# The layout of a transposed K tile: where the stride goes, into the copy or into the weight load

## The chip, the core and the metric

The kernel runs on one core of a Trainium2 chip. The metric is the device time of one execution in microseconds (us), the median of several runs. The profile of one execution stands beside it.

## The reference, cut to what matters

Two blocks, one behind the other. The first is a gated linear attention with complex gates, over 4 batches, 8 heads, 768 positions and 48 channels a head:

```python
scale = np.minimum(mag, 0.999) / (mag + 1e-06)      # mag = |a_re + i a_im|
for t in range(S):
    S_re, S_im = ar*S_re - ai*S_im + kv, ar*S_im + ai*S_re   # kv = k_t (outer) v_t
    y[:, :, t] = q_t @ S_re
```

The second is a multiplicative feed-forward block on the 3072 rows of 384 values that this gives: `h = ((x @ w1) * (x @ w2)) @ w3`, and `h @ w_out`. All is fp32.

## The kernel before, in words

**Units.** The 768 positions of a batch are cut in two halves of 384 (TT), so there are 8 units (NU). A unit has three chunks (UC) of 128 positions (C).

**Gates.** `gates(u)` computes the running products of the gates' magnitudes and the running sums of their angles by scans, and multiplies q and k with them. It leaves two tensors of rotated k: R holds the real part and K2 the imaginary part. In both, a partition is a pair (d, head), with 16 values of d and 8 heads side by side, and a column block f (three of them, KD) tells which third of a head's 48 channels is meant. From the same data, DMAs build QL and KL, which have the 96 values (d, real or imaginary, f) of one head down the partitions.

**States.** For a chunk's contribution to the state, the positions must lie down the partitions. `turn(u, c, x)` transposes the three blocks of R (x = 0) or K2 (x = 1) for chunk c on TensorE into one PSUM tile `tp` of 128 positions by (f, d, head), and ScalarE copies this into the SBUF tile KT (L654). Then `state(u, c)` multiplies, for each head, the 96 columns of KT that belong to it (the weights, 128 positions by 96) with 64 columns of V (the moving operand), into the PSUM tile `kv` (L702), and adds the state before to it (L707 or L709). The profile shows two instructions of a kind for each fp32 matmul or weight load of this product: a group of 8 heads is 16 loads and 16 matmuls. Where the state is needed further, `turn` and `state` are called for all three chunks of an even unit and for two of an odd one: 5 chunks for each batch, 20 in all, and 40 copies, one for each chunk and x.

**Outputs and feed-forward.** `scores` (L664) and `outputs` (L691) give the chunk's part of y, which is copied to `xT` (L693). `ffn_ab` multiplies xT with w1 and w2 (L722), and `ffn_out` (L738) multiplies their product with the fused matrix w3 w_out, which L852 makes at the start.

**Order.** TensorE's order is written by hand: `unit` and `pieces` deal the attention pieces of unit u out among the feed-forward matmuls of unit u - 1. The other engines' order comes from a scheduler; the copies of L654, L693, L727 have high priority in it. The unit's transposes come first, and a chunk's `state` comes one piece behind the second of its transposes.

**The layout that matters here.** KT is laid out before as (head, d, x, f). A head's 96 columns lie together, so the weight load of L702 reads 96 elements in a row. The copy of L654 goes through `tp` in its own order (f, d, head), the head innermost. In KT a step of one head is 96 elements, so every element of the write lies 384 bytes from the one before it.

Of the kernel before, what the change touches and what calls it, by code (L numbers as in the profile page):

```python
# [10 lines left out]
FP = mybir.dt.float32  # L11
# [363 lines left out]
def kernel(  # L375
# [36 lines left out]
    nc = tc.nc  # L412
    B, H, D, S = qt.shape
    P = 128
# [4 lines left out]
    KD = DM // P  # L419
    DG = P // H  # L420
# [25 lines left out]
    two = fast.enter_context(tc.tile_pool(name="two", bufs=2))  # L446
# [33 lines left out]
    g_t, L_t, xT_t, ab_t, T_t, KT_t = {}, {}, {}, {}, {}, {}  # L480
# [164 lines left out]
    def turn(u, c, x):  # L645

        src = L_t[u][2 + x]
        if x == 0:
            KT_t[u, c] = two.tile([P, H, DG, 2, KD], FP, tag="KT", name="KT")
        tp = ps_v.tile([P, KD, C], FP, tag="v", name="tp")  # L650
        for f in range(KD):
            nc.tensor.transpose(out=tp[:, f], in_=src[:, f, c * C:(c + 1) * C], identity=ident)  # L652
        with tc.high_priority():
            nc.scalar.copy(out=KT_t[u, c][:, :, :, x].rearrange("p h d f -> p f d h"),  # L654
                           in_=tp.rearrange("p f (d h) -> p f d h", h=H))

    def scores(u, c, x):
# [37 lines left out]
    def state(u, c):  # L695

        KT, V = KT_t.pop((u, c)), Vb[u % 2][:, c]
        n = u % 2 * UC + c
        T = T_t.get((u // 2, n))
        kv = ps_v.tile([2 * D, H, 64], FP, tag="v", name="kv")  # L700
        for hd in range(H):
            nc.tensor.matmul(out=kv[:, hd], lhsT=KT[:, hd].rearrange("p d x f -> p (d x f)"), rhs=V[:, hd],  # L702
                             start=True, stop=True)
        Tn = three.tile([2 * D, H, 64], FP, tag="T", name="T")
        with tc.high_priority():
            if T is None:
                nc.scalar.copy(out=Tn, in_=kv)  # L707
            else:
                nc.vector.tensor_tensor(out=Tn, in0=kv, in1=T, op=OP.add)  # L709
        if c == UC - 1:  # L710
            rho = L_t[u][1][:, :, TT:TT + 1].to_broadcast([2 * D, H, 64])
            nc.vector.tensor_tensor(out=Tn, in0=Tn, in1=rho, op=OP.mult)
        T_t[u // 2, n + 1] = Tn
# [170 lines left out]
    def pieces(u):  # L884

        sc = [[lambda c=c, x=x: scores(u, c, x) for x in range(2)] for c in range(UC)]
        tr = [[lambda c=c, x=x: turn(u, c, x) for x in range(2)] for c in range(UC)]
        kv = [lambda c=c: state(u, c) for c in range(UC)]
        y = [lambda c=c: outputs(u, c) for c in range(UC)]

        if u % 2:
            return [[tr[0][0]], [tr[0][1]], [tr[1][0], kv[0]], [tr[1][1]], [kv[1]], sc[0], sc[1] + [y[0]], sc[2] + [y[1]],
                    [y[2]]]
        return [[tr[0][0]], [tr[0][1]], [tr[1][0], kv[0]], [tr[1][1]], [tr[2][0], kv[1]], [tr[2][1]], [kv[2]] + sc[0],
                sc[1] + [y[0]], sc[2] + [y[1]], [y[2]]]
# [131 lines left out]
```

## Time and profile before

| what | value |
|---|---|
| time, median of 3 runs | 591.22 us (587.91 to 591.81) |
| span of the profiled execution | 591.2 us |
| TensorE busy | 556.7 us |
| ScalarE busy | 350.2 us |
| VectorE busy | 304.7 us |
| clock granted to TensorE, mean | 0.98 |

The profile's names: PE is TensorE, PEld its weight loads, which run beside the matmuls, ACT is ScalarE, DVE is VectorE, SPq the queue that issues the DMAs. L654 is line 654 of the kernel. A group row gives the line, the engine, the operation, the tiles (out<-in) and their shapes, the count, then the busy time in us, the mean of one in ns, and the engine's idle time just before with what ended it. The mean of one instruction on TensorE includes latency that the next one overlaps, so the pace of a row of matmuls is read from the chain of waits, in which each piece starts where the one that released it ends.

### The profile page before, as it was taken

The numbers are of one execution on the slowest core, as the hardware profiler recorded it, in microseconds if no ns is written. First come the engines' busy times: TensorE is split into PE (matmuls) and PEld (weight loads), VectorE is DVE, ScalarE is ACT, GpSimd is POOL, SyncE is SP. The second block draws the span as 40 slices with busy tenths as digits, with TensorE's granted clock in tenths as the row PEclk, the third lists the DMA queues.
The fourth block names the chain that finished last, engine by engine and source line by source line (L and its number), as shares of the span: only waits on it lengthen the run. The fifth ranks groups of instructions, "written<-read, shape, count | busy, mean of one in ns | idle before, by whom it ended". The sixth has DMA issues, their size and how long they took to land.

```text
span 591.2 us, 8844 instructions
## 1 busy us (share of the span) xinstructions
PE 556.7 (94%) x3514; PEld 367.3 (62%) x3514; DVE 304.7 (52%) x420; ACT 350.2 (59%) x572; POOL 5.3 (1%) x11
## 2 busy tenths in 40 slices
PE   4779989979899999999999999999999999999996
PEld 2335775558456765677567765776567756766553
DVE  6998488845761576158512674257415682300110
ACT  6897648566983698379835698498635742111100
POOL 3000000000000000000000000000000000000000
PEclk9779999989899999999999999999999999999999
DMA  8777999377385648652754347825920026000001
GB/s 294 271 280 221 250 287 287 108 183 213 121 234 117 185 137 240 130 173 85 194 120 105 124 141 177 247 73 157 206 76 1 14 67 121 1 15 29 0 1 44
DMA packets 46050, 84.71 MB, mean 143 GB/s; under 512 B 4656, under 2 KB 36144, under 8 KB 45104
## 3 DMA queue, kind: packets, MB, share of 16 engines
q1 hardware_dynamic: 46000, 84.06, 50.2%
q8 instruction: 29, 0.48, 0.3%
q14 instruction: 21, 0.17, 0.1%
HBM read 60.42 MB, written 4.72 MB: 110 GB/s over the span
## 4 chain that ended last, share of the span: by engine, by line
PE 66%; DMA 10%; ACT 9%; DVE 8%; SPq 4%; issue 2%; DVEq 0%; ACTq 0%
PE m L722 38%; PE o L738 13%; PE y L691 4%; PE sc L664 3%; PE f L852 3%; SPq L485 3%; PE kv L702 3%; DMA im<-in_a_im_dram 2%; ACT gZ L544 2%; DMA look<-in_w_dram 2%; PE tp L652 2%; DMA look<-in_a_re_dram 2%; DMA raw<-in_w_dram 1%; DMA vr<-in_v_dram 1%; ACT re L544 1%
## 5 line engine op out<-in xcount | busy, mean ns | idle before, releaser
L722 PE MATMUL m<-xT,w1s 128*128 128x384 f32 x384 | 136.4, 492 | 3.6 <-ACT xT L693 3.6
L722 PE MATMUL m<-xT,w2s 128*128 128x384 f32 x384 | 134.9, 488 | 1.0 <-ACT a L727 0.5
L738 PE MATMUL o<-w3o,ab 128*128 128x384 f32 x384 | 131.2, 495 | 0.0
L728 DVE TENSOR_TENSOR ab<-m,a 128x384 f32<-128x384 f32 x64 | 35.5, 556 | 140.4 <-PE m L722 131.9
L722 PEld LDWEIGHTS m<-xT,w2s 128*128 128x128 f32 x384 | 73.2, 191 | 53.1 <-ACT a L727 1.2
L738 PEld LDWEIGHTS o<-w3o,ab 128*128 128x128 f32 x384 | 71.7, 192 | 49.0 <-issue 4.9
L722 PEld LDWEIGHTS m<-xT,w1s 128*128 128x128 f32 x384 | 70.7, 191 | 47.3 <-ACT xT L693 5.1
L727 ACT COPY a<-m 128x384 f32<-128x384 f32 x64 | 30.4, 475 | 75.8 <-PE m L722 75.8
L852 PE MATMUL f<-wo_s,w3s 128*128 128x384 f32 x128 | 49.7, 548 | 17.8 <-DVE wo_s L775 17.8
L654 ACT COPY KT<-tp 128x384 f32<-128x384 f32 x40 | 33.6, 846 | 43.4 <-PE tp L652 43.4
L852 PEld LDWEIGHTS f<-wo_s,w3s 128*128 128x128 f32 x128 | 27.0, 217 | 37.8 <-DVE wo_s L775 19.6
L664 PE MATMUL sc<-QL,KL 96*128 96x128 f32 x384 | 47.8, 278 | 2.2 <-DVE A L666 2.2
L664 PEld LDWEIGHTS sc<-QL,KL 96*128 96x128 f32 x384 | 45.6, 192 | 6.1 <-DVE A L666 3.5
L666 DVE COPY_PREDICATED A<-causal,sc 128x512 f32<-128x512 int32 x48 | 34.2, 734 | 15.4 <-PE sc L664 15.0
L691 PE MATMUL y<-A,V 128*32 128x128 f32 x768 | 39.2, 275 | 0.0
L691 PEld LDWEIGHTS y<-A,V 128*32 128x32 f32 x768 | 32.8, 109 | 5.7 <-issue 2.2
L691 PE MATMUL y<-QL,T 96*32 96x128 f32 x640 | 34.4, 272 | 0.0
L742 ACT COPY ot<-o 128x384 f32<-128x384 f32 x24 | 11.2, 465 | 35.2 <-PE o L738 35.2
L702 PEld LDWEIGHTS kv<-V,KT 128*96 128x96 f32 x320 | 29.6, 165 | 3.2 <-issue 2.0
L691 PEld LDWEIGHTS y<-QL,T 96*32 96x32 f32 x640 | 31.2, 110 | 0.0
L702 PE MATMUL kv<-V,KT 128*96 128x64 f32 x320 | 29.9, 246 | 0.7 <-ACT KT L654 0.7
L544 ACT ACTIVATE re<-gZ 128x1152 int32<-128x1152 f32 (+3 forms) x20 | 19.1, 964 | 15.1 <-DVE gZ L600 13.5
(98 smaller groups left out, 585.3 us busy)
## 6 DMA issues: line engine op xcount, KB each, us to landing
look<-in_w_dram SPq DMA_DIRECT2D x28, 512.0 KB, 4.7
raw<-in_w_dram SPq DMA_DIRECT2D x7, 1024.0 KB, 8.2
raw<-in_w_dram SPq DMA_DIRECT2D x8, 768.0 KB, 8.0
KL<-gR SPq DMA_DIRECT2D x24, 192.5 KB, 3.2
KL<-k SPq DMA_DIRECT2D x24, 192.5 KB, 3.7
re<-in_a_re_dram SPq DMA_DIRECT2D x24, 192.0 KB, 5.8
im<-in_a_im_dram SPq DMA_DIRECT2D x24, 192.0 KB, 3.4
k<-in_k_dram SPq DMA_DIRECT2D x24, 192.0 KB, 3.5
```

Of the source, the lines that this page charges most:

```text
L485: queue.dma_start(out=dst[:, i, 0:TT], in_=src[b, :, DG * f:DG * (f + 1), h * TT:(h + 1) * TT].rearrange("h d s -> d h s"))
L544: chain(nc.scalar.activation(**kw))
L654: nc.scalar.copy(out=KT_t[u, c][:, :, :, x].rearrange("p h d f -> p f d h"), in_=tp.rearrange("p f (d h) -> p f d h", h=H))
L664: nc.tensor.matmul(out=sc[:, j], lhsT=KL[:, x * n + j, w], rhs=QL[:, x * n + j, w], start=True, stop=True)
L666: nc.vector.copy_predicated(out=A[:, x * n:(x + 1) * n], data=sc, mask=causal.rearrange("p (h t) -> p h t", h=1).to_broadcast([P, n, C]))
L691: nc.tensor.matmul(out=o, lhsT=a, rhs=b, start=s0, stop=s1)
L702: nc.tensor.matmul(out=kv[:, hd], lhsT=KT[:, hd].rearrange("p d x f -> p (d x f)"), rhs=V[:, hd], start=True, stop=True)
L722: nc.tensor.matmul(out=m, lhsT=w[:, j * P // WB, f, j * P % WB:j * P % WB + P], rhs=xT_t[u][:, f], start=(f == 0), stop=(f == KD - 1))
L727: nc.scalar.copy(out=a, in_=got[0])
L728: nc.vector.tensor_tensor(out=ab_t[u][:, j], in0=got[1], in1=a, op=OP.mult)
L738: nc.tensor.matmul(out=m, lhsT=ab_t[u][:, f, t * P:(t + 1) * P], rhs=w3o[:, f], start=(f == 0), stop=(f == KF - 1))
L852: nc.tensor.matmul(out=sums[j], lhsT=w3_t[f][:, j * P:(j + 1) * P], rhs=w3_t["wo"][:, f], start=(f == 0), stop=(f == KF - 1))
```

## The change

KT is laid out as (d, x, f, head), with the eight heads of a channel side by side. The copy of L654 then writes runs of eight elements (32 bytes) where it wrote single elements, which is what the change is for. The price is on the other side: the 96 columns of a head are now eight elements apart, and the weight load of L702 reads them at a stride of 32 bytes. The order of the 96 columns is the same as before, and so are the size of the tile, its buffers, the number of instructions and their order.

```diff
         if x == 0:
-            KT_t[u, c] = two.tile([P, H, DG, 2, KD], FP, tag="KT", name="KT")
+            KT_t[u, c] = two.tile([P, DG, 2, KD, H], FP, tag="KT", name="KT")
         tp = ps_v.tile([P, KD, C], FP, tag="v", name="tp")
         for f in range(KD):
             nc.tensor.transpose(out=tp[:, f], in_=src[:, f, c * C:(c + 1) * C], identity=ident)
         with tc.high_priority():
-            nc.scalar.copy(out=KT_t[u, c][:, :, :, x].rearrange("p h d f -> p f d h"),
+            nc.scalar.copy(out=KT_t[u, c][:, :, x].rearrange("p d f h -> p f d h"),
                            in_=tp.rearrange("p f (d h) -> p f d h", h=H))
...
         for hd in range(H):
-            nc.tensor.matmul(out=kv[:, hd], lhsT=KT[:, hd].rearrange("p d x f -> p (d x f)"), rhs=V[:, hd],
+            nc.tensor.matmul(out=kv[:, hd], lhsT=KT.rearrange("p d x f h -> p (d x f h)")[:, hd::H], rhs=V[:, hd],
                              start=True, stop=True)
```

## The prediction

> **What bounds the kernel now.** I read the page first for the shares of the engines, then the chain of waits, the groups of the two instructions that change, what TensorE waits for, and last a table of stretches, which tells where TensorE has idle time that could be won or could swallow something. The page:
>
> ```profile
> PE 556.7 (94%) x3514; PEld 367.3 (62%) x3514; DVE 304.7 (52%) x420; ACT 350.2 (59%) x572; POOL 5.3 (1%) x11
> ...
> PE   4779989979899999999999999999999999999996
> ```
>
> TensorE is busy in nine tenths or more of nearly every slice after the first quarter. ScalarE, whose copy the change is meant to shorten, is busy 59% of the span. A piece of the chain of waits, late in the run (start, us, what):
>
> ```profile
> 424.92 3.87 PE m L722 x12
> 428.79 0.33 PE tp L652 x3
> 429.12 3.87 PE m L722 x12
> 432.99 0.33 PE tp L652 x3
> 433.32 1.33 PE kv L702 x16
> 434.65 0.33 PE tp L652 x3
> 434.98 3.87 PE m L722 x12
> ```
>
> The chain is TensorE's own queue: one group starts as the one before it ends, and the copy of L654 isn't in it, though it runs between its transpose and its kv group. Sixteen kv matmuls take 1.33 us, 83 ns each; twelve matmuls that stream 384 columns take 3.87 us, 322 ns each (0.84 ns a column). A kv matmul streams only 64 columns (54 ns at that rate), but loads 96 columns of weights. So the kv group is set by its weight loads, not by what it streams. The groups (busy us, mean ns, idle before and its releaser):
>
> ```profile
> L727 ACT COPY a<-m 128x384 f32<-128x384 f32 x64 | 30.4, 475 | 75.8 <-PE m L722 75.8
> L654 ACT COPY KT<-tp 128x384 f32<-128x384 f32 x40 | 33.6, 846 | 43.4 <-PE tp L652 43.4
> L702 PEld LDWEIGHTS kv<-V,KT 128*96 128x96 f32 x320 | 29.6, 165 | 3.2 <-issue 2.0
> L702 PE MATMUL kv<-V,KT 128*96 128x64 f32 x320 | 29.9, 246 | 0.7 <-ACT KT L654 0.7
> ```
>
> Two copies of 128x384 from PSUM: contiguous 475 ns, with runs of one element at a stride of 96 elements (384 bytes) 846 ns. The waits of TensorE from 62 us on, that is from the first transpose:
>
> ```profile
> PE tp L652 <- DVE gR L616: 3.6, 1, 3.6
> PE m L722 <- ACT xT L693: 3.6, 3, 2.5
> PE sc L664 <- DVE A L666: 2.2, 5, 1.0
> PE kv L702 <- ACT KT L654: 0.7, 1, 0.7
> ```
>
> Of all its waits, one of 0.7 us is for the copy that gets faster. Stretches of the span (busy us and instructions of PE, PEld, DVE, ACT, POOL; clock; DMA):
>
> ```profile
> 62.00:86.00 24.00, 21.86 (x291) 18.59 (x290) 14.66 (x22) 14.23 (x21) 0.00 (x0) 1.00 1.08 258
> 86.00:158.00 72.00, 64.72 (x429) 42.66 (x430) 47.69 (x58) 49.90 (x86) 0.00 (x0) 0.98 0.69 197
> 158.00:217.00 59.00, 58.70 (x368) 39.51 (x371) 32.00 (x39) 42.01 (x68) 0.00 (x0) 0.97 0.60 166
> 430.00:505.00 75.00, 74.70 (x470) 50.24 (x469) 35.72 (x53) 34.60 (x50) 0.00 (x0) 1.00 0.20 48
> ```
>
> TensorE lies idle 2.1 + 7.3 = 9.4 us between 62 and 158 us, and 0.3 us in each of the two later stretches shown. Whatever lengthens its queue after 158 us lengthens the kernel by as much.
>
> **What the Trainium skill says.** Three places bear on this. "SBUF — State Buffer", section Specifications (TRN2), gives 16-byte cachelines and says that at least two hits on a line are needed for full bandwidth, each move to a new line costing something. A stride of eight fp32 is 32 bytes, one hit to a line. The trace agrees for ScalarE's writes (846 ns against 475 ns, one hit to a line against four); for TensorE's reads no instruction in it has a stride, so nothing shows it. "TensorE: Matmul & The Clock Gate", section LDWEIGHTS (loading the stationary operand), prices a load at its columns divided by 1.2 per ns: 96 columns are 80 ns. The chain has 83 ns for each kv matmul, so it agrees, and says again that loads bound this group. "ScalarE: Activation LUTs", section What ACT_TABLE_LOAD costs, gives 186 ns + 0.833 ns an element, 506 ns for 384; the trace has 475 ns, and that is used.
>
> **The copies, L654.** The write becomes runs of eight elements, 32 bytes, two full lines with four hits each; the PSUM side is read in order as before. No copy with runs of eight is in the trace. Bounds: 475 ns (as the contiguous one) and 846 ns (no gain). I take 475 ns. That removes 40 x (846 - 475) = 14.8 us from ScalarE. What lies beside it: TensorE runs ffn matmuls between a transpose and the kv group (3.87 us in the chain above against a copy of 0.85), so the copy is hidden, except for the one wait of 0.7 us. Its ScalarE queue neighbours also run up to 0.37 us sooner for each copy ahead of them, and those feed 3.6 us of TensorE's waits (the xT copy). The gain on the path is 0.7 us, and at most the 0.7 + 3.6 = 4.3 us of these waits.
>
> **The weight loads, L702.** 20 states x 8 heads are 160 calls, and the trace has 320 loads: two to a call. Each now takes 96 elements at 32 bytes apart. The low bound is no change, 80 ns. The nearest row is the copy of L654, where an element that comes alone to its line costs (846 - 475) / 384 = 0.97 ns more; on 96 elements that is +93 ns. A plain halving of the rate is +80 ns. I take the middle, +87 ns, so that a kv group goes from 16 x 83 = 1.33 us to about 2.7 us. The sum is 320 x 87 = 27.8 us on TensorE (25.6 to 29.8). Nothing can hide within the group: a load runs beside the matmul before it, but that streams for 54 ns only. Behind the group stand the next transposes, ffn matmuls and scores, all in one queue.
>
> Of this, five of the twenty groups stand before 158 us, where the idle time is, and add 5 x 16 x 87 ns = 7.0 us there. The idle time that follows a kv group is the waits of the scores for the mask copy (2.2 us) and of the ffn for xT (3.6 us). I let about half of these waits, 3 us, swallow that much of the added time: an estimate, as the waits partly move along when TensorE is late. The fifteen later groups add 20.9 us in full.
>
> **The tile.** KT has the same size and buffers in both shapes, and every engine has the same instructions in the same order, with the same waits. No wait is added; the order of the weights' columns (channel, real or imaginary, block) stays, so T and what reads it do not change.
>
> **The sum.** 591.2 + 27.8 - 3 - 0.7 = 615.3 us.
>
> **Rivals.**
>
> 1. The strided load costs nothing, since TensorE takes an fp32 weight only every 0.83 ns. For it: elements of ScalarE's reads at a stride of two (L805, 679 ns for 512 and 567 ns for 384, 0.88 ns an element) run nearly at the contiguous rate. Against it: these have two elements to a line, and the only accesses with one to a line are slow. Then what is left is the copy's 0.7 us and a little of the xT waits: 591.2 - 1 = 590 us.
> 2. The other side, faster by over 1%: loads are free, and ScalarE's 14.8 us pull the gates of units 1 and 2 forward, whose chain TensorE waits for between 86 and 158 us. For it: ScalarE is busy 49.9 of these 72 us. Against it: only four of the forty copies (3.4 us, of which 1.5 us would be saved) stand in that stretch, and much of its chain is DMA. All 4.3 us gone, and a little more of the idle time, would be 586 us or less.
> 3. A load of another size: half the penalty (+40 ns, 12.8 us less 3 swallowed and 0.7 won: 600 us), where part of the load is latency that a stride leaves alone, or three times the load (+160 ns, 51.2 us: 639 us), where each line costs more on this port. The trace speaks for neither.
>
> **How the numbers follow.** A load at about twice its time has 0.60: the written rule and the one measured single-hit access agree, but the measured one is a write on another engine. Rival 1 has 0.25, rival 2 has 0.08, rival 3 has 0.07 in all. The forecast is the likeliest, 615 us. The range must hold rival 1, or it would leave out a third: it goes from 587 us, just above rival 2, to 621 us, where the whole 29.8 us are added and nothing is swallowed. The chances: faster 0.08 (rival 2), same 0.25 (rival 1, and 597 us is the border), slower 0.67 (the forecast and rival 3).
>
> **What would show it.** In the changed profile: the copies of L654 near 475 ns (right) or above 600 ns (runs of eight don't fill lines); the mean of a kv load well above 165 ns, 245 to 260 ns, since that row seems to hold some 85 ns beside the 80 ns of streaming; a kv group of 16 at 2.6 to 2.8 us in the chain instead of 1.33 us, and PE kv L702 at over 5% of the chain instead of 2.9%; stretches after 158 us longer by 1.4 us for each kv group in them; ScalarE's busy time near 335 us. The prediction is wrong if the kv group still takes 1.33 us: then the time stays, whatever the copies do. It is also wrong if the load is slower and the span isn't, which would mean that TensorE's queue isn't the path that I take it for.

## The result and the profile after

The changed kernel takes 615.42 us (median of 4 runs, 614.78 to 616.1) against 590.85 us before in the same rounds: 24.6 us more, a ratio of 1.0417 (95% interval 1.0377 to 1.0456). The forecast of 615 us, slower by 4%, was right. The page after:

```profile
PE 583.2 (95%) x3514; PEld 395.7 (65%) x3514; DVE 304.8 (50%) x420; ACT 336.6 (55%) x572; POOL 5.3 (1%) x11
...
PE   4769999899999999999999999999999999999996
```

TensorE has 26.5 us more of busy time for the same 3514 matmuls, and ScalarE 13.6 us less. The groups of the kernel after, to be laid beside those of before (busy us, mean ns, idle before and its releaser):

```profile
L727 ACT COPY a<-m 128x384 f32<-128x384 f32 x64 | 30.4, 475 | 100.1 <-PE m L722 100.1
L702 PEld LDWEIGHTS kv<-V,KT 128*96 128x96 f32 x320 | 59.6, 275 | 2.1 <-issue 0.5
L702 PE MATMUL kv<-V,KT 128*96 128x64 f32 x320 | 59.2, 338 | 0.3 <-ACT KT L654 0.3
L654 ACT COPY KT<-tp 128x384 f32<-128x384 f32 x40 | 19.0, 479 | 46.9 <-PE tp L652 46.9
```

The copy went from 846 to 479 ns, nearly the 475 ns of a contiguous one (L727). The loads and the kv matmuls, and no other group, are busy twice as long as before: 29.3 us more for the matmuls. The chain of waits in the same place as the piece shown of before:

```profile
443.73 3.87 PE m L722 x12
447.61 0.33 PE tp L652 x3
447.93 2.82 PE kv L702 x16
450.75 0.33 PE tp L652 x3
451.09 3.87 PE m L722 x12
454.96 0.33 PE tp L652 x3
455.29 2.82 PE kv L702 x16
```

The ffn groups keep their 3.87 us and the transposes their 0.33 us; a kv group takes 2.82 us in place of 1.33 us. That is 176 ns a matmul, 93 ns more. What TensorE waits for in the stretch of units 0 and 1, 61 to 160 us (total us, times, longest):

```profile
PE tp L652 <- DVE gR L616: 1.9, 1, 1.9
PE m L722 <- ACT xT L693: 0.8, 2, 0.6
PE tp L652 <- ACT w3o L856: 0.4, 1, 0.4
PE kv L702 <- ACT KT L654: 0.3, 1, 0.3
PE sc L664 <- DVE A L666: 0.3, 1, 0.3
```

That stretch in the table by time (the columns are those of the table in the prediction):

```profile
61.50:160.00 98.50, 95.16 (x722) 69.23 (x722) 63.70 (x78) 62.70 (x107) 0.00 (x0) 0.98 0.75 207
```

TensorE is idle for 98.5 - 95.2 = 3.3 us here. Before, it was idle for 98.5 - 88.9 = 9.6 us in the same stretch, with these waits for xT and for the mask beside the 3.6 us for gR that the prediction shows:

```profile
PE m L722 <- ACT xT L693: 3.4, 2, 2.5
PE sc L664 <- DVE A L666: 1.3, 2, 1.0
```

Part of the longer groups went into time that TensorE would have waited anyway.

### The profile page after: what moved, and what is told of

It reads as the page before. It is cut to its first block, busy times and chain, and to the rows that moved or that the text cites. A ratio compares the mean times of both kernels' runs of the same rounds, so it can differ in the third digit from the quotient of the medians.

```text
span 613.2 us, 8844 instructions
## 1 busy us (share of the span) xinstructions
PE 583.2 (95%) x3514; PEld 395.7 (65%) x3514; DVE 304.8 (50%) x420; ACT 336.6 (55%) x572; POOL 5.3 (1%) x11
## 4 chain that ended last, share of the span: by engine, by line
PE 73%; DVE 10%; ACT 8%; DMA 5%; issue 2%; SPq 1%; ACTq 0%; DVEq 0%
PE m L722 33%; PE o L738 18%; PE kv L702 9%; PE sc L664 5%; PE y L691 5%; PE tp L652 2%; DMA raw<-in_w_dram 2%; ACT re L544 1%; ACT gZ L544 1%; DMA vr<-in_v_dram 1%; DVE gZ L600 1%; PE f L852 1%; ACT gR L544 1%; DMA look<-in_w_dram 1%; DMA k<-in_k_dram 1%
## 5 line engine op out<-in xcount | busy, mean ns | idle before, releaser
L722 PE MATMUL m<-xT,w1s 128*128 128x384 f32 x384 | 135.0, 488 | 0.8 <-ACT xT L693 0.8
L727 ACT COPY a<-m 128x384 f32<-128x384 f32 x64 | 30.4, 475 | 100.1 <-PE m L722 100.1
L702 PEld LDWEIGHTS kv<-V,KT 128*96 128x96 f32 x320 | 59.6, 275 | 2.1 <-issue 0.5
L702 PE MATMUL kv<-V,KT 128*96 128x64 f32 x320 | 59.2, 338 | 0.3 <-ACT KT L654 0.3
L654 ACT COPY KT<-tp 128x384 f32<-128x384 f32 x40 | 19.0, 479 | 46.9 <-PE tp L652 46.9
L709 DVE TENSOR_TENSOR T<-kv,T 96x512 f32<-96x512 f32 x16 | 11.0, 687 | 49.2 <-PE kv L702 49.2
```

The source lines that it names most:

```text
L654: nc.scalar.copy(out=KT_t[u, c][:, :, x].rearrange("p d f h -> p f d h"), in_=tp.rearrange("p f (d h) -> p f d h", h=H))
L702: nc.tensor.matmul(out=kv[:, hd], lhsT=KT.rearrange("p d x f h -> p (d x f h)")[:, hd::H], rhs=V[:, hd], start=True, stop=True)
L722: nc.tensor.matmul(out=m, lhsT=w[:, j * P // WB, f, j * P % WB:j * P % WB + P], rhs=xT_t[u][:, f], start=(f == 0), stop=(f == KD - 1))
L727: nc.scalar.copy(out=a, in_=got[0])
```

## The experiments

The theory: a weight read at 32 bytes from the one before it is alone in its 16-byte line and takes about twice the time; the kv groups are bound by their loads, so all of that is TensorE's, and the shorter copy gives nothing back. The rivals: the loss comes from the new copy or needs it; any stride costs, or larger ones cost more; a slow load holds TensorE up in itself, not only where nothing hides it.

### The load alone

```diff
-lhsT=KT[:, hd].rearrange("p d x f -> p (d x f)")
+lhsT=KT.rearrange("p h d x f -> p (h d x f)")[:, hd::H]
```

> KT and its copy as before the change; only the weight load reads at a stride of eight (so it reads other values of KT: the kv products are not those of the reference). Theory (the whole loss is the weight load, one element to a 16-byte line): a kv group of 16 takes 2.8 us in the chain, the copies stay at 846 ns, and the time is that of the changed kernel or up to 1 us more, 615 to 617 us. Rival (the loss needs the new copy too, for instance since KT is written in another pattern beside the loads): the time stays near 591 us, or the loss is clearly smaller than 24 us.

Measured: 616.56 us against 591.07 us, a ratio of 1.0423 (1.0387 to 1.046). The first groups of the chain:

```profile
64.92 2.82 PE kv L702 x16
69.70 2.82 PE kv L702 x16
```

The copies, in the groups:

```profile
L654 ACT COPY KT<-tp 128x384 f32<-128x384 f32 x40 | 33.7, 848 | 44.7 <-PE tp L652 44.7
```

The copies are the slow ones of before, the groups the slow ones of after, and the loss is there in full: the rival, by which it needs the new copy, is out. It needs nothing but the stride of the read.

### The copy alone

```diff
-KT_t[u, c] = two.tile([P, H, DG, 2, KD], FP, tag="KT", name="KT")
+KT_t[u, c] = two.tile([P, DG, 2, KD, H], FP, tag="KT", name="KT")
...
-out=KT_t[u, c][:, :, :, x].rearrange("p h d f -> p f d h")
+out=KT_t[u, c][:, :, x].rearrange("p d f h -> p f d h")
...
-lhsT=KT[:, hd].rearrange("p d x f -> p (d x f)")
+lhsT=KT.rearrange("p d x f h -> p (d x f h)")[:, 96 * hd:96 * (hd + 1)]
```

> KT and its copy as after the change; the weight load reads 96 elements in a row (so other values than a head's: the kv products are not those of the reference). Theory: copies at 479 ns, a kv group at 1.33 us, ScalarE 14.7 us less busy, and the time 589.5 to 591 us, since the copy was hidden: 0.7 us to win and little more. Rival (14.7 us of ScalarE pull the gates forward, which TensorE waits for between 62 and 158 us): 586 us or less.

Measured: 591.28 us against 591.07 us, a ratio of 1.0001 (0.9986 to 1.0016), with the copies and kv groups as expected. Two groups of its chain:

```profile
176.90 1.33 PE kv L702 x16
182.77 1.33 PE kv L702 x16
```

Its copies:

```profile
L654 ACT COPY KT<-tp 128x384 f32<-128x384 f32 x40 | 19.0, 478 | 46.0 <-PE tp L652 45.8
```

ScalarE has 13.6 us less to do (336.6 against 350.2 us busy) and the time doesn't move: ScalarE goes on waiting for TensorE. The 0.7 us that was forecast for the copy is within the interval (0.12% of 591 us), and so is nothing at all. The rival of 586 us is out.

### How the cost depends on the stride

Three kernels. In one, of which there is a single profiled execution and no time to compare, unit u reads its weights at a stride of u + 1 elements:

```diff
-lhsT=KT[:, hd].rearrange("p d x f -> p (d x f)")
+lhsT=KT.rearrange("p h d x f -> p (h d x f)")[:, 0:96 * (u + 1):u + 1]
```

> As before the change, but the weight load of unit u reads KT at a stride of u + 1 elements, one to eight (other values than a head's: the kv products are not those of the reference). A look at the loads unit by unit. Theory (16-byte lines, at least two hits each for the full rate): groups of 1.33 us for strides one and two, a value between for three (12 bytes, a line is hit once or twice), and 2.8 us alike for four to eight. Rival (cost grows with the stride): a rising row, with eight the worst. Rival (a power of two is what hurts): 2.8 us at four and eight, less at five, six and seven.

One kv group of each unit from 2 to 7 in its chain, so the strides three to eight in this order:

```profile
176.57 2.04 PE kv L702 x16
...
242.52 2.77 PE kv L702 x16
...
307.50 2.61 PE kv L702 x16
...
376.04 2.61 PE kv L702 x16
...
440.71 2.72 PE kv L702 x16
...
508.63 2.82 PE kv L702 x16
```

A step at four and then a plateau, as the theory has it and the rival of a rising row doesn't. The rival of powers of two falls too, as the cause of the step: five, six and seven stand within 8% of four and eight. At a stride of two, the second group of unit 1 takes 1.39 us from its start to that of the next piece, a little over the 1.33 us expected. For the price of an element: 384 streamed columns take 3.87 us / 12 = 322 ns, and the 256 of a kernel further below 3.45 us / 16 = 216 ns. That is 0.83 ns for each further column, and some 2.5 ns are left over for each matmul. I take the same two numbers for the load, as 96 x 0.83 + 2.5 ns gives the 83 ns of a row. With one element alone in each line, five or six apart, an element of a load takes (2.61 us / 16 - 2.5 ns) / 96 = 1.67 ns, twice 0.83. At three, twelve bytes, four elements lie in three lines; if a line costs at least two steps of 0.83 ns, that is 1.5 steps an element, 120 ns a load, and the group gives 2.04 us / 16 - 2.5 ns = 125 ns. The model of two steps a line is a reading that fits, within 8%. Four and eight are 6 to 8% above five and six, and seven is 4% above; what makes that part is not settled.

The other two compute the reference in full, with two or four heads of a channel side by side (N is 2 or 4):

```diff
-KT_t[u, c] = two.tile([P, H, DG, 2, KD], FP, tag="KT", name="KT")
+KT_t[u, c] = two.tile([P, H // N, DG, 2, KD, N], FP, tag="KT", name="KT")
...
-out=KT_t[u, c][:, :, :, x].rearrange("p h d f -> p f d h"),
-in_=tp.rearrange("p f (d h) -> p f d h", h=H)
+out=KT_t[u, c][:, :, :, x].rearrange("p g d f n -> p f d g n"),
+in_=tp.rearrange("p f (d g n) -> p f d g n", g=H // N, n=N)
...
-lhsT=KT[:, hd].rearrange("p d x f -> p (d x f)")
+lhsT=KT[:, hd // N].rearrange("p d x f n -> p (d x f n)")[:, hd % N::N]
```

> KT kept with two heads of a channel side by side: copies write runs of two (8 bytes), weights are read at a stride of two (8 bytes), the reference is computed in full. Theory (a line of 16 bytes, two hits to it are enough): loads as before (165 ns, kv group 1.33 us) and copies near 480 ns, time 589.5 to 591 us. Rival (every stride other than one slows the load, by the same step): kv group 2.8 us and 615 us. Rival (the cost grows with the stride): a group of 1.5 us or so and 594 us.

> KT kept with four heads of a channel side by side: copies write runs of four (16 bytes, a whole line), weights are read at a stride of four (16 bytes); the reference is computed in full. Theory (one element to a line, as at eight; the curve gave 2.7 us a group): kv group 2.7 to 2.77 us, copies near 480 ns, time 613 to 615 us. Rival (what counts is the distance, so half of the stride is half of the loss): about 603 us.

Pairs: 591.94 us against 591.07 us, a ratio of 1.0015 (1.0002 to 1.0029). Fours: 614.18 us against 590.88 us, 1.0379 (1.0344 to 1.0414). A group of the chain with pairs, one of the chain with fours, and the copies of the pairs:

```profile
179.40 1.39 PE kv L702 x16
```

```profile
180.25 2.77 PE kv L702 x16
```

```profile
L654 ACT COPY KT<-tp 128x384 f32<-128x384 f32 x40 | 20.3, 509 | 45.2 <-PE tp L652 45.1
```

With pairs both ends are nearly free: the copy, which writes runs of two elements, has 509 ns, and a load, whose elements lie eight bytes apart, costs (1.39 - 1.33) us / 16 = 4 ns more, which is 320 x 4 ns = 1.2 us, about the 0.9 us that the pairs lost (0.1 to 1.7 us). I had expected exactly the old group time here. The rivals for the pairs (2.8 us and 615 us, or 1.5 us and 594 us) are out. With fours, the copy takes 478 ns, and the load pays almost all at sixteen bytes that it pays at thirty-two. The rival that distance counts (603 us) is out. The pairs get nearly all of the copy's gain and lose almost none of the load's; since the copy's gain is worth nothing here, they don't beat the kernel before either.

### The stream in place of the load

```diff
-rhs=V[:, hd],
+rhs=V.rearrange("p h e -> p (h e)")[:, 0:64 * (u + 1):u + 1],
```

> As before the change, but the streamed operand of the kv products, 64 columns of V, is read at a stride of u + 1 elements in unit u, one to eight (other values than a head's: the kv products are not those of the reference); the weights lie in a row. Theory (the line rule holds for this read as for the load; streaming is hidden under the 80 ns load until it grows past it): a group of 16 stays at 1.33 us for strides one and two, rises to about 1.7 us for three (64 x 1.56 cycles of 0.83 ns is 83 ns) or stays, and is 1.9 to 2.0 us from four on (64 x 1.81 ns is 116 ns, 16 of these and the 2.5 ns are 1.9 us). Rival (only the weight path pays): 1.33 us at every stride.

Again there is one profiled execution. Groups with the streamed operand at strides of one, three, four and eight (units 0, 2, 3 and 7):

```profile
65.13 1.33 PE kv L702 x16
...
180.18 1.41 PE kv L702 x16
...
244.22 1.85 PE kv L702 x16
...
502.16 1.89 PE kv L702 x16
```

The streamed side pays the same toll: 1.89 us / 16 - 2.5 ns is 116 ns for 64 columns, 1.81 ns each, where the strided load has 2.82 us / 16 - 2.5 ns = 174 ns for 96, 1.81 ns each. The rival, by which only the weights pay, is out. From five to eight the groups take 1.87 to 1.89 us: the dip of the load at five and six isn't there. Here only what goes past the 80 ns of the load is seen. At three, the first of the two guesses (1.7 us) missed; the sum that stood beside it gives 16 x (83 + 2.5) ns = 1.37 us, and 1.41 us is measured. At four, 1.85 us lies just under the 1.9 to 2.0 us forecast. Reading K as the stream and V as the weights should therefore not evade the stride; that was not run.

### The load under a longer stream

Both layouts again, but each kv product streams 256 columns over its weights:

```diff
-nc.tensor.matmul(out=kv[:, hd], lhsT=..., rhs=V[:, hd],
+nc.tensor.matmul(out=kv[:, hd // 4 * 4:hd // 4 * 4 + 4], lhsT=..., rhs=V[:, hd // 4 * 4:hd // 4 * 4 + 4],
```

> As before the change, but each kv product streams 256 columns of V (four heads') over its 96 weights, so that each streams for longer than a load at either stride takes; later products overwrite earlier ones, and the kv values are not those of the reference. Theory: a kv group of 16 takes 16 x (256 x 0.833 + 2.5) = 3.45 us whatever the load. Against the kernel before that is 20 x 2.1 = 42 us of TensorE and, with 5 to 6 us of idle time swallowed, some 627 to 633 us. This is the other half of the pair with the wide strided kernel.

> As after the change, with the same 256 columns for each kv product as the wide kernel that reads its weights in a row; the kv values are not those of the reference. Theory (the stride only costs where the load is longer than the stream of the matmul before it): loads still 275 ns or so, but a kv group 3.45 us, and the time within 1 us of the other wide kernel, where the change itself costs 24.6 us. Rival (a strided load holds TensorE up, whatever runs beside it): a group near 5 us, and the time 25 us above the other wide kernel.

Measured: 627.26 us with weights in a row, 627.66 us with weights eight apart; against 591.28 us before, ratios of 1.0604 (1.0579 to 1.0628) and 1.0611 (1.0586 to 1.0637). The loads, in a row and then eight apart:

```profile
L702 PEld LDWEIGHTS kv<-V,KT 128*96 128x96 f32 x320 | 51.5, 163 | 18.7 <-issue 2.7 <-ACT KT L654 0.3
```

```profile
L702 PEld LDWEIGHTS kv<-V,KT 128*96 128x96 f32 x320 | 69.7, 255 | 2.6 <-issue 1.0
```

The groups of unit 2 in the two chains, in the same order:

```profile
184.28 3.45 PE kv L702 x16
192.26 3.45 PE kv L702 x16
203.79 3.47 PE kv L702 x16
```

```profile
183.23 3.52 PE kv L702 x16
191.27 3.52 PE kv L702 x16
202.86 3.47 PE kv L702 x16
```

The loads are slow still (255 ns against 163 ns), and the loss is gone: 0.4 us between the two kernels, where the change itself costs 24.6 us. The rival (a group near 5 us) is out. The two kernels differ in their copies as well, but the copy alone was worth nothing that could be measured. The 0.07 us left over in two of the three groups fits the first load of each: it stands behind a transpose, whose pace is 110 ns (0.33 us for three), against a load of 174 ns. The third group stands behind ffn matmuls of 322 ns and shows nothing. So what costs is the load beyond the stream before it.

### Which groups count

The change in units 0 and 1 only, and in units 2 to 7 only; for the second, `u >= 2` stands in place of `u < 2` (KT is a flat tile, and each unit takes the layout of before or after):

```diff
-lhsT=KT[:, hd].rearrange("p d x f -> p (d x f)")
+lhsT=KT[:, hd::H] if u < 2 else KT[:, 96 * hd:96 * (hd + 1)]
```

> The change in units 0 and 1 alone, five of the twenty kv groups; the reference is computed in full. They add 5 x 1.49 = 7.4 us to TensorE, in the stretch that held 9.4 us of its idle time. By the prediction's estimate 3 us of it are swallowed and 0.7 won: 591 + 3.7 = 595 us. By the trace of the changed kernel, where this idle time is 6 us shorter: 592.5 us. If nothing were swallowed: 598 us.

> The change in units 2 to 7 alone, fifteen of the twenty kv groups; the reference is computed in full. They stand where TensorE has no idle time: 15 x 1.49 = 22.3 us, all of it seen, 613 to 614 us. If this stretch too could swallow some: clearly below 612 us.

Measured: 593.22 us for the first two units, 1.004 (1.0027 to 1.0053), and 612.33 us for the rest, 1.0351 (1.032 to 1.0383), both against 590.88 us. The five groups of the first kernel and its sixth (line 704 is L702 of the others):

```profile
64.49 2.82 PE kv L704 x16
69.27 2.82 PE kv L704 x16
73.72 2.76 PE kv L704 x16
126.70 3.11 PE kv L704 x16
136.59 2.75 PE kv L704 x16
181.22 1.33 PE kv L704 x16
```

The fourth comes just behind a wait for its KT, so nothing runs beside its first load. In the second kernel, a group of unit 0 and the first of unit 2:

```profile
68.20 1.33 PE kv L704 x16
177.40 2.82 PE kv L704 x16
```

The first five grow by about 7.4 us and the time by 2.3 us (1.6 to 3.1 us): some 5.1 us are swallowed, more than the 3 us forecast and a little less than the 6 us that I read from the trace. The fifteen later groups add 21.4 us (about 2 us either way) of the 22.3 us. Six of them come behind ffn matmuls and take 2.75 or 2.76 us, so their sum is nearer 21.9 us; the time lies a little under the 613 to 614 us forecast for that reason, or by the noise. The two parts sum to 23.8 us, the change measured 24.6 us.

The idle time of one stretch isn't all there is to read. In the traces of before, of the copy alone and of the later units alone, the last wait for xT, at 152 to 158 us, is 2.5 to 2.6 us long, and the twelve ffn matmuls behind it take 5.5 to 5.7 us; the clock granted to TensorE between 158 and 162 us of the trace before is 0.57. In the changed kernel and in that of the first two units, this wait is 0.2 us, and the twelve take 4.0 us (the changed kernel's clock there is 1.00). But these two then wait 1.4 us for gR of unit 2, just past the stretch, and the other three do not, so what they won there is mostly given back. The slow matmuls aren't explained by the wait alone: behind a wait of 2.3 us in the kernel with pairs, the twelve take 4.0 us.

## Why the prediction was right, step by step

- **What bounds the kernel.** Right, and shown from both sides: 13.6 us taken from ScalarE moved nothing (the copy alone), and some 22 us added to TensorE after 158 us came out as 21.4 us (the later units alone).
- **The copies.** 475 ns taken, 479 ns measured; ScalarE's busy time 335 us forecast, 336.6 us measured. Its worth on the path, 0.7 us, can't be told from zero, neither in the copy alone nor between the load alone (1.0423) and the whole change (1.0417).
- **The load.** +87 ns taken, from bounds of +80 and +93; the groups give +93 ns. Twice the time was the right mechanism; the middle of the two bounds had no other ground than to split them. The value carried over from ScalarE's write (0.97 ns more an element, 1.80 in all) was the better one: the load has 1.81. "SBUF — State Buffer", section Specifications (TRN2), asks for at least two hits on a 16-byte line; no trace showed that for TensorE when the forecast was made, and now the steps at three and four do.
- **Nothing hides within the group.** Right: a group grows by 1.49 us, 93 ns for each of its 16 loads. The wide pair shows the reason, as the same loads cost nothing behind a long stream. "TensorE: Matmul & The Clock Gate", section LDWEIGHTS (loading the stationary operand), has 80 ns for 96 columns; that holds for a row (83 ns a matmul measured) and not for a stride of eight (176 ns).
- **What the idle time swallows.** 3 us estimated, about 5 us measured in the run with the first two units alone. This term was mis-sized, and the load's by 2 us the other way (29.8 us measured against 27.8): the two errors cancel, and that 615.3 us came within 0.2 us of the measured time is luck. The estimate took half of two waits; between 61 and 160 us the trace after shows the wait for xT falling from 3.4 to 0.8 us, the mask's from 1.3 to 0.3 us, and the one for gR, which the estimate had left out, from 3.6 to 1.9 us. The waits for xT and gR are as short in the two other kernels with these groups longer (the load alone, the first two units) and stay at 3.1 us or more in the two without (the copy alone, the later units). The mask's wait is 0.3 us in the copy alone too, so its fall can't be put down to the longer groups.
- **A sign that missed.** The mean of a load was forecast at 245 to 260 ns and is 275 ns: the row rose by 110 ns where the pace of the groups fell back by 93. The row of a pipelined instruction isn't its price; the chain is.

## What to carry to other kernels

A layout that moves a stride from one access to another should be priced at both ends, and by which end the path runs through: here 370 ns less for each of 40 hidden copies met 93 ns more for each of 320 exposed loads. Compare a group's load time with what the matmul before it streams, for that says how much of a slower load is hidden and how much is paid. If the fp32 weights of a load must lie apart, eight bytes was nearly free here, and sixteen cost almost as much as thirty-two; for the copy, runs of two elements were already nearly as fast as a contiguous write.

## What the runs showed of the hardware

The toll for one fp32 element alone in its line came out alike, 1.80 to 1.81 ns against 0.83 ns in a row, in three kinds of access: ScalarE's write (at 384 bytes), TensorE's weight load and its streamed operand (both at 32 bytes). I hadn't expected a write on one engine to price a read on another that closely. At strides of five and six elements the load is a little cheaper, 1.67 ns, than at four, seven and eight (1.78, 1.75 and 1.81 ns); the streamed operand, at 1.77 to 1.81 ns from four to eight, doesn't show this.
